# A fused attention and squared-ReLU block: activation sums on DVE alone, one product of seven by one step, and small products in the order of their weight blocks

## The chip, the core and the metric

The kernel runs on one core of a Trainium2 chip. The core has a matrix engine (PE, which loads weights and streams columns past them), a vector engine (DVE), an activation engine (ACT), a general engine (GpSimd, POOL in the profile) and a queue engine (SP) that issues nearly all transfers of this kernel. Each engine works through its own instructions in order and waits on semaphores for the others. The metric is the time of one execution on the device in microseconds, the median of several runs; lower is better.

## The reference

Attention without softmax, a norm, then a two-matrix block with a squared ReLU, all in float32:

```python
kv = np.einsum('bhsd,bhse->bhde', k, v)            # batch 8, heads 8, seq 576, head_dim 64
out = np.einsum('bhsd,bhde->bhse', q, kv)
rms = np.sqrt(np.mean(out * out, axis=-1, keepdims=True) + 1e-06)
x = (out / rms * g_norm)                           # to (4608 tokens, 512)
h = x @ w_in                                       # 512 x 2048
r = np.maximum(h, 0.0)
g = r * r
return g @ w_out                                   # 2048 x 512
```

## The kernel before

**Strips.** The 4608 tokens are 36 tiles of 128; four tiles make a strip, nine strips in all (0 to 8). Each strip has an up stage (x times W_in, ReLU, square, giving g) and a down stage (g times W_out). Slices of the attention for later strips (`attend`) are interleaved with the up stages. Program order is the order of each engine; nothing is reordered by a scheduler.

**Fast products.** A product of 2 x 2 blocks is made from seven block products P1 to P7 instead of eight (Winograd's form of Strassen), at the price of sums on either side. Strip 0 computes its up stage plainly; all others use seven products for each of four groups of columns (`up`). The down stage uses seven products in every strip. In strips 0 and 1 each of them is done by `down` in two halves of 8 matmuls on 256 columns. From strip 2 on (`DEEP` = 2) each of the seven is itself split into seven small products (`down_deep`, L753): two levels, 49 small products of four 128 x 128 x 128 matmuls. A float32 matmul stands as two instructions in the profile, so an outer product is 7 x 4 x 2 = 56 instructions there.

**A deep down stage.** The outer products run in the order 4, 1, 2, 6, 5, 7, 3. Product p needs:

- a quarter of g (`gq`, tile `gt`, 128 x 2048): quarters 11, 12, 21, 22. P4 and P5 read 22, P1 and P6 read 11, P2 and P3 read 21, P7 reads 12. Between products three of them are overwritten with the outer sums: 22 becomes 12 + 22 behind P4 (L764, DVE), 12 becomes 11 - 12 (L765, GpSimd), 11 becomes 22 - 11 behind P1 (L767, DVE), 21 becomes 21 - 11 behind P2 (L768, GpSimd).
- four leaf sums (`leaf_sums`, L707, tiles `g_s`, 128 x 512, DVE): s1 = a21 + a22, s2 = s1 - a11, s3 = a11 - a21, s4 = a12 - s2. Small products 1, 2 and 4 read quarters of the quarter as they are; 5, 6, 7, 3 read s1, s2, s3, s4.
- two blocks of weights, streamed by SP into a ring of four buffers (`stream`, L630): first the columns for small products 3, 1, 2, out of `w_out` (768 KB, L639), then those for 5, 6, 7, 4, out of `w_deep` (1 MB, L644). The ring is reused as PE releases a buffer.

The small products of one p are issued in two halves, (1, 2, 4) and then (5, 6, 7, 3) (L793). They accumulate in two PSUM banks, a chain: "A" for P1, P6, P7 and "B" (banks C and B) for P4, P2, P5, P3. P6, P7 and P3 go on accumulating onto the product before them in their chain. After the first half of product k, `together` (L736) adds the banks of product k - 1 into an output tile: one copy on ACT, then four adds on DVE reading PSUM, and where an output quarter is complete, one more add and the stores (`send`, L650), eight small DMAs on SP for most strips. Then the leaf sums for product k + 1 follow on DVE. Only after the second half are the blocks of two products ahead requested (`stream(2)`, L774), behind any stores in SP's order.

**Strip 0.** At the first down step (L806) the buffers of the weight conversion become those of the sums, `sums_g` (L576) for all four groups is issued (a sum for P5 and a difference for P7 each), and then the steps P1, P2, P5, P6, P7, P3, P4 run, with normalizations (`query`, `normalized`, L401) and transposes (`features`, L448) of later tiles between them. The difference for P6 is issued behind P1 (L674), that for P3 behind P2 (L678).

Of the kernel before, what the change touches and what calls it, by code (L numbers as in the profile page):

```python
# [14 lines left out]
ALU = mybir.AluOpType  # L15
# [4 lines left out]
def kernel(  # L20
# [34 lines left out]
    nc = tc.nc  # L55
    P = 128
    B, H, S, D = q.shape
# [5 lines left out]
    C = S // P  # L63
# [7 lines left out]
    N_STRIP = N_TILE // NT  # L71
# [168 lines left out]
    def minus(eng, out, a, b):  # L240
        eng.tensor_tensor(out=out, in0=a, in1=b, op=ALU.subtract)  # L241
# [235 lines left out]
    def sums_x(s):  # L477
        xc[s] = t1, t2, t3, t4 = [
            sum_pool.tile([P, TH // SQ, KH, SQ], FP32, name=f"x_t{i}", tag="sum") for i in range(4)
        ]  # L480
        x = lambda kh, th: halves(s, kh, th)
        minus(nc.vector, t1, x(0, 1), x(0, 0))
        minus(nc.vector, t2, x(1, 1), t1)
        minus(nc.vector, t3, x(1, 1), x(0, 1))
        minus(nc.vector, t4, x(1, 0), t2)
# [138 lines left out]
        w_blk[0, p] = t.rearrange("p f (h e) -> p h f e", h=2)  # L624
    DEEP_ORDER = (4, 1, 2, 6, 5, 7, 3)
    to_stream = [(s, p) for s in range(DEEP) for p in ORDER if (s, p) not in w_blk]
    to_stream += [(s, p, n) for s in range(DEEP, N_STRIP) for p in DEEP_ORDER for n in range(2)]
    to_stream = iter(to_stream)

    def stream(n=1):  # L630
        for _, u in zip(range(n), to_stream):
            s, p = u[:2]
            t = stream_pool.tile([P, 4, FQ // 2, P], FP32, name="w_blk", tag="w_blk")
            if s < DEEP:
                w_blk[u] = t.rearrange("p (h a) f e -> p h (a f) e", h=2)
                nc.sync.dma_start(out=w_blk[u], in_=w_out[B_OUT[p]])
            elif u[2] == 0:

                nc.sync.dma_start(  # L639
                    out=t[:, 1:4], in_=w_out[B_OUT[p]].rearrange("p h (a f) e -> p (h a) f e", a=2)[:, 1:4]  # L640
                )
                w_blk[s, p, 3], w_blk[s, p, 1], w_blk[s, p, 2] = (t[:, i] for i in range(1, 4))
            else:
                nc.sync.dma_start(out=t, in_=w_deep[B_OUT[p]])  # L644
                w_blk[s, p, 5], w_blk[s, p, 6], w_blk[s, p, 7], w_blk[s, p, 4] = (t[:, i] for i in range(4))

    def out_tile():
        return c_pool.tile([P, 2, DH], FP32, name="o_sb", tag="c")
# [6 lines left out]
    def down(s, p, i):  # L655
        if i == 0:
            open_bank(p)
        a = {1: 11, 2: 21, 6: 11, 7: 12, 3: 21, 4: 22}.get(p)
        w = w_blk[s, p]
        product(  # L660
            p, i,
            lambda fc: (gq[s, 1, fc // 2][:, fc % 2] if p == 5 else gq[s, a][:, fc])[:, ts(i, P)],
            lambda fc: w[:, :, fc], FQ,
        )
        if i == 0:
            if s == DEEP - 1:
# [24 lines left out]
        combine(p, store(0, 0), store(0, 1), store(1, 0), store(1, 1))  # L691
# [15 lines left out]
    def leaf_sums(s, p):  # L707
        a = gq[s, A_G[p]]
        a11, a12, a21, a22 = (a[:, ts(f, FQ // 2), ts(t, P)] for t in range(2) for f in range(2))
        s1, s2, s3, s4 = (sum_pool.tile([P, FQ // 2, P], FP32, name=f"g_s{i}", tag="sum") for i in range(4))  # L710
        leaf[p] = {1: a11, 2: a12, 3: s4, 4: a22, 5: s1, 6: s2, 7: s3}
        nc.vector.tensor_tensor(out=s1, in0=a21, in1=a22, op=ALU.add)  # L712
        minus(nc.vector, s2, s1, a11)
        minus(nc.vector, s3, a11, a21)
        minus(nc.vector, s4, a12, s2)


    PLACE = {1: (0, 0), 2: (0, 1), 6: (0, 2), 5: (1, 0), 7: (1, 1), 3: (1, 2), 4: (1, 3)}

    def small_products(s, p, js):  # L720
        c = "B" if p in (4, 2, 5, 3) else "A"
        if js[0] == 1 and p not in (6, 7, 3):
            chain[c] = [
                fpsum.tile([P, 4, P], FP32, name=f"ps_{c}", tag=t, bufs=2 if t == "A" else 1)
                for t in ("AA" if c == "A" else "CB")
            ]
        for j in js:
            x, i = PLACE[j]
            a, w = leaf[p][j], w_blk.pop((s, p, j))
            for f in range(FQ // 2):  # L730
                nc.tensor.matmul(  # L731
                    chain[c][x][:, i, :], lhsT=a[:, f, :], rhs=w[:, f, :],
                    start=p not in (6, 7, 3) and j in (1, 4) and f == 0, stop=f == FQ // 2 - 1, skip_group_check=True,
                )

    def together(p):  # L736

        x, y = chain["B" if p in (4, 2, 5, 3) else "A"]
# [3 lines left out]
        add = lambda out, a, b: nc.vector.tensor_tensor(out=out, in0=a, in1=b, op=ALU.add)  # L742
# [6 lines left out]
        for a, th, eh in {2: [(1, 0, 0)], 7: [(4, 1, 0), (5, 1, 1)], 3: [(6, 0, 1)]}.get(p, []):  # L749
            add(part[a], part[a], o)  # L750
            send(s, th, eh, part[a])

    def down_deep(s, k, js):  # L753
        p = DEEP_ORDER[k]
        small_products(s, p, js)
        before = DEEP_ORDER[k - 1] if k else None
        after = DEEP_ORDER[k + 1] if k < 6 else None
        g = lambda q: gq[s, q]
        if js[0] == 1:
            if k:  # L760
                together(before)
            if k == 0:
                leaf_sums(s, after)
                nc.vector.tensor_tensor(out=g(22), in0=g(12), in1=g(22), op=ALU.add)  # L764
# [12 lines left out]

    attend(ready[0] - 2)
    for i in range(NP, NP + 2):
# [2 lines left out]
    for s in range(N_STRIP):  # L782
# [6 lines left out]
        if s < DEEP:  # L789

            steps += [(2, down, (s, p, i)) for p in (ORDER if s else (1, 2, 5, 6, 7, 3, 4)) for i in range(2)]
        else:
            steps += [(2, down_deep, (s, k, js)) for k in range(7) for js in ((1, 2, 4), (5, 6, 7, 3))]  # L793
        goal = ready.get(s + 1, len(slices))
        total, done = sum(w for w, _, _ in steps), 0
        for i, (w, fn, a) in enumerate(steps):
            if s == 0 and i < n_up:

                convert(5 + (3 * i + 2) // 4)
                if i in (2, 4):  # L800
                    load_next()
                if i == 3:
                    load_q_rest(0, nc.sync)
                    load_rest(1, nc.sync)
                    load_q_rest(1, nc.sync)
# [12 lines left out]
            fn(*a)  # L818
            done += w
            if s:  # L820
# [52 lines left out]
```

## Time and profile before

| | us |
|---|---|
| median of 3 runs (1011.82 to 1011.95) | 1011.83 |
| the profiled execution | 1007.17 |
| its span, first to last instruction | 1005.4 |
| PE busy | 937.5 (93%) |
| DVE busy | 684.7 (68%) |
| ACT busy | 230.5 (23%) |
| GpSimd busy | 67.9 (7%) |

All times in views are microseconds from the start of the span. Busy time counts an instruction from its start to its modelled end; consecutive matmuls overlap, so start-to-start distances tell more than durations. A row of a wait names the engine that waited, what released it, the total, the times and the longest. The mean granted PE clock of the execution is 0.983 of full speed.

### The profile page before, as it was taken

How to read it: one execution, taken by the hardware profiler on the slowest of the kernel's cores; microseconds unless marked ns; L12 is line 12 of the kernel's file. 1: busy time of each engine (PE TensorE's matmuls, PEld its weight loads, DVE VectorE, ACT ScalarE, POOL GpSimd, SP SyncE). 2: the span in 40 equal slices, each digit the busy share in tenths (PEclk: the TensorE clock that was granted, in tenths of full speed). 3: DMA queues.
4: the chain of work that ended last, by engine and by line, in shares of the span. 5: the costliest groups of instructions: out<-in, count | busy, mean ns of one | idle time of the engine just before them, and what ended most of it. 6: DMA issues, size and time to landing. Idle time of an engine off the chain costs nothing.

```text
span 1005.4 us, 15784 instructions
## 1 busy us (share of the span) xinstructions
PE 937.5 (93%) x6144; PEld 828.0 (82%) x6144; DVE 684.7 (68%) x1203; ACT 230.5 (23%) x508; POOL 67.9 (7%) x21
## 2 busy tenths in 40 slices
PE   3699899999999999998999899989998999989995
PEld 3344788888889988898889888979898989988995
DVE  3899754585448974697569774986479557953593
ACT  3798241320022002200230022101220122002200
POOL 0000000000000300030002100110002000300030
PEclk9899999999999999999999999999999999989998
DMA  8699862546973566566555656466416721662064
GB/s 255 219 298 296 280 197 93 121 142 212 323 218 86 220 247 187 121 222 243 169 134 182 239 188 163 142 234 221 117 59 217 260 83 47 225 248 78 13 226 170
DMA packets 165530, 185.86 MB, mean 185 GB/s; under 512 B 85200, under 2 KB 138960, under 8 KB 156880
## 3 DMA queue, kind: packets, MB, share of 16 engines
q1 hardware_dynamic: 165296, 184.86, 57.2%
q8 instruction: 48, 0.79, 0.3%
q14 instruction: 26, 0.21, 0.1%
q10 hardware_dynamic: 160, 0.00, 0.0%
HBM read 153.62 MB, written 31.20 MB: 184 GB/s over the span
## 4 chain that ended last, share of the span: by engine, by line
PE 66%; DVE 23%; DMA 6%; issue 2%; ACT 2%; SPq 1%; DVEq 0%
PE ps_A L552 25%; PE ps_B L552 12%; DVE g_s L241 8%; PE ps_C L552 7%; PE ps_B L731 7%; PE ps_A L731 6%; DVE g_s L712 4%; DVE o_sb L742 3%; PE ps_A L588 2%; PE x_ps L378 2%; DMA w_blk<-w_out 2%; PE kv_ps L349 2%; DVE gt L241 2%; DVE gt L764 2%; DMA w_blk<-w_deep 1%
## 5 line engine op out<-in xcount | busy, mean ns | idle before, releaser
L552 PE MATMUL ps_A<-x_t,w_in 128*128 128x256 f32 x768 | 182.6, 381 | 1.3 <-DVE gt L611 1.3
L552 PEld LDWEIGHTS ps_A<-x_t,w_in 128*128 128x128 f32 x768 | 143.6, 190 | 21.1 <-DVE gt L611 2.1
L241 POOL TENSOR_TENSOR gt<-gt 128x2048 f32<-128x2048 f32 x14 | 66.2, 4726 | 902.0 <-DVE gt L764 856.6
L731 PE MATMUL ps_B<-w_blk,g_s 128*128 128x128 f32 x896 | 104.6, 275 | 0.0
L731 PEld LDWEIGHTS ps_B<-w_blk,g_s 128*128 128x128 f32 x896 | 102.3, 192 | 0.0
L731 PE MATMUL ps_A<-w_blk,gt 128*128 128x128 f32 x504 | 68.2, 297 | 21.6 <-DMA w_blk<-w_out 20.1
L731 PE MATMUL ps_A<-w_blk,g_s 128*128 128x128 f32 x672 | 80.5, 276 | 7.9 <-DVE g_s L241 7.9
L731 PEld LDWEIGHTS ps_A<-w_blk,g_s 128*128 128x128 f32 x672 | 77.5, 192 | 9.2 <-DVE g_s L241 9.2
L731 PEld LDWEIGHTS ps_A<-w_blk,gt 128*128 128x128 f32 x504 | 65.3, 211 | 23.2 <-issue 21.2
L731 PE MATMUL ps_B<-w_blk,gt 128*128 128x128 f32 x672 | 79.6, 275 | 0.0
L731 PEld LDWEIGHTS ps_B<-w_blk,gt 128*128 128x128 f32 x672 | 77.9, 192 | 0.4
L612 DVE SCALAR_TENSOR_TENSOR gt<-gt 128x512 f32<-128x512 f32 x96 | 66.4, 692 | 3.3
L562 ACT COPY snap<-ps_A 128x512 f32<-128x512 f32 x68 | 39.7, 584 | 116.9 <-PE ps_A L552 110.3
L241 DVE TENSOR_TENSOR g_s<-g_s,gt 128x512 f32<-128x512 f32 x49 | 63.3, 1291 | 1.7
L611 DVE TENSOR_TENSOR gt<-ps_C,snap 128x512 f32<-128x512 f32 x32 | 21.9, 684 | 60.6 <-PE ps_C L552 60.6
L611 DVE TENSOR_TENSOR gt<-ps_A,snap 128x512 f32<-128x512 f32 x32 | 22.0, 687 | 59.6 <-PE ps_A L552 59.5
L552 PE MATMUL ps_A<-xT,w_in 128*128 128x256 f32 x256 | 61.2, 382 | 0.0
L552 PE MATMUL ps_C<-xT,w_in 128*128 128x256 f32 x256 | 61.0, 381 | 0.0
L552 PE MATMUL ps_B<-x_t,w_in 128*128 128x256 f32 x256 | 60.9, 381 | 0.0
L552 PE MATMUL ps_B<-xT,w_in 128*128 128x256 f32 x256 | 60.7, 380 | 0.0
L742 DVE TENSOR_TENSOR o_sb<-o_sb,ps_A 128x256 f32<-128x256 f32 (+1 forms) x84 | 32.4, 386 | 38.8 <-ACT o_sb L743 28.4
L712 DVE TENSOR_TENSOR g_s<-gt 128x512 f32<-128x512 f32 x49 | 54.5, 1112 | 0.5
(118 smaller groups left out, 1284.5 us busy)
## 6 DMA issues: line engine op xcount, KB each, us to landing
w_blk<-w_deep SPq DMA_DIRECT2D x49, 1024.0 KB, 7.2
w_blk<-w_out SPq DMA_DIRECT2D x49, 768.0 KB, 4.5
w_blk<-w_out SPq DMA_DIRECT2D x11, 1024.0 KB, 6.4
raw<-in_moe_w_in_dram SPq DMA_DIRECT2D x16, 512.0 KB, 6.3
raw<-in_moe_w_out_dram SPq DMA_DIRECT2D x16, 512.0 KB, 5.1
k<-in_k_dram SPq DMA_DIRECT2D x30, 256.0 KB, 3.0
v<-in_v_dram SPq DMA_DIRECT2D x30, 256.0 KB, 3.3
w_deep<-w_t SPq DMA_DIRECT2D x7, 1024.0 KB, 8.5
```

The lines of the kernel that those rows point to most:

```text
L241: eng.tensor_tensor(out=out, in0=a, in1=b, op=ALU.subtract)
L349: nc.tensor.matmul(ps[ts(h, D)], lhsT=a, rhs=w, start=c == 0, stop=c == C)
L378: nc.tensor.matmul(o, lhsT=qT[b, p][:, c_b, :], rhs=kvd[b, p], start=True, stop=True)
L552: nc.tensor.matmul(bank[BANK[p]][:, i, :], lhsT=lhsT(k), rhs=rhs(k), start=p in (1, 5, 2) and i == 0 and k == 0, stop=k == n - 1, skip_gro ...
L562: nc.scalar.copy(snap[p], b)
L588: nc.tensor.matmul(ps, lhsT=w_in[:, kc % KH, g, kc // KH * 2 + fh, ts(i, P)], rhs=xt[0][:, :, kc, :], start=kc == 0, stop=kc == NP - 1,)
L611: nc.vector.tensor_tensor(out=o, in0=b, in1=a, op=ALU.add)
L612: nc.vector.scalar_tensor_tensor(out=o, in0=o, scalar=0.0, in1=o, op0=ALU.max, op1=ALU.mult)
L712: nc.vector.tensor_tensor(out=s1, in0=a21, in1=a22, op=ALU.add)
L731: nc.tensor.matmul(chain[c][x][:, i, :], lhsT=a[:, f, :], rhs=w[:, f, :], start=p not in (6, 7, 3) and j in (1, 4) and f == 0, stop=f == F ...
L742: add = lambda out, a, b: nc.vector.tensor_tensor(out=out, in0=a, in1=b, op=ALU.add)
L764: nc.vector.tensor_tensor(out=g(22), in0=g(12), in1=g(22), op=ALU.add)
```

## The change

1. `DEEP_ORDER` stays, but P2 is no longer split: it is done as in strips 0 and 1, by one step, 16 matmuls on 256 columns into bank C. Its weights come as one block of 1 MB from `w_out`; its four leaf sums and its `together` fall away, and its result is added to P1's output tile from bank C directly.
2. The two GpSimd subtractions are issued on DVE: 12 one product later than before (behind the combination of P4, at P1), 21 at P6.
3. The halves are (1, 2, 3) and (4, 5, 6, 7), so each half reads one block only. After every half the next load is requested, one at a time. In `leaf_sums`, s4 is computed ahead of s3. The sum for quarter 22 is issued behind the second half of P4.
4. In strip 0 the four `sums_g` are issued one in front of each of the first four down steps; the difference for P6 moves behind P2, that for P3 behind P5.

```diff
-    to_stream += [(s, p, n) for s in range(DEEP, N_STRIP) for p in DEEP_ORDER for n in range(2)]
+    for s in range(DEEP, N_STRIP):
+        for p in DEEP_ORDER:
+            to_stream += [(s, p, n) for n in range(2)] if p != 2 else [(s, p)]
...
-        if p == 1:
+
+        if p == (1 if s else 2):
             for g in range(NG):
                 x = gq[s, 11][:, ts(g, 2)]
                 minus(nc.vector, x, gq[s, 1, g], x)
-        if p == 2:
+        if p == (2 if s else 5):
             minus(nc.vector, gq[s, 21], gq[s, 21], gq[s, 11])
...
         minus(nc.vector, s2, s1, a11)
+        minus(nc.vector, s4, a12, s2)
         minus(nc.vector, s3, a11, a21)
-        minus(nc.vector, s4, a12, s2)
...
-        c = "B" if p in (4, 2, 5, 3) else "A"
+        c = "B" if p in (4, 5, 3) else "A"
...
-    def down_deep(s, k, js):
+    def down_deep(s, k, i):
         p = DEEP_ORDER[k]
-        small_products(s, p, js)
-        before = DEEP_ORDER[k - 1] if k else None
-        after = DEEP_ORDER[k + 1] if k < 6 else None
-        g = lambda q: gq[s, q]
-        if js[0] == 1:
-            if k:
-                together(before)
-            if k == 0:
-                leaf_sums(s, after)
-                nc.vector.tensor_tensor(out=g(22), in0=g(12), in1=g(22), op=ALU.add)
-                minus(nc.gpsimd, g(12), g(11), g(12))
-            if k == 2:
-                minus(nc.vector, g(11), g(22), g(11))
-                minus(nc.gpsimd, g(21), g(21), g(11))
-            if 0 < k < 6:
-                leaf_sums(s, after)
-            if k == 6 and s + 1 < N_STRIP:
-                sums_x(s + 1)
-        else:
-            stream(2)
+        if p == 2:
+            if i == 0:
+                open_bank(p)
+            w = w_blk[s, p]
+            product(p, i, lambda fc: gq[s, 21][:, fc, ts(i, P)], lambda fc: w[:, :, fc], FQ)
+        else:
+            small_products(s, p, ((1, 2, 3), (4, 5, 6, 7))[i])
+        if p != 2 or i == 1:
+            stream()
+        q11, q12, q21, q22 = (gq[s, q] for q in (11, 12, 21, 22))
+        if i == 1:
+            if k == 0:
+                nc.vector.tensor_tensor(out=q22, in0=q12, in1=q22, op=ALU.add)
             if k == 6:
-                together(p)
+                together(s, p)
+            return
+        if k == 3:
+            c11 = part[1]
+            nc.vector.tensor_tensor(out=c11, in0=c11, in1=bank["C"], op=ALU.add)
+            send(s, 0, 0, c11)
+        elif k:
+            together(s, DEEP_ORDER[k - 1])
+        if k == 0:
+            leaf_sums(s, 1)
+        if k == 1:
+            minus(nc.vector, q12, q11, q12)
+        if k == 2:
+            minus(nc.vector, q11, q22, q11)
+        if 2 <= k < 6:
+            leaf_sums(s, DEEP_ORDER[k + 1])
+        if k == 3:
+            minus(nc.vector, q21, q21, q11)
+        if k == 6 and s + 1 < N_STRIP:
+            sums_x(s + 1)
...
                 stream(3)
-                for g in range(NG):
-                    sums_g(0, g)
...
+            if s == 0 and n_up <= i < n_up + NG:
+                sums_g(0, i - n_up)
             fn(*a)
```

What the change moves stands in the order of the program at three places.

**PE, the first deep strip, product P1** (`w_blk_1920` is its block from `w_out`, `w_blk_1922` that from `w_deep`; `g_s0` to `g_s3` are s1 to s4). Before:

```order
L731 MATMUL ps_A_2378<-w_blk_1920,gt_1929 128x128 x8
L731 MATMUL ps_A_2379<-w_blk_1922,gt_1929 128x128 x4
L731 MATMUL ps_A_2379<-w_blk_1922,g_s0_2348 128x128 x4
L731 MATMUL ps_A_2378<-w_blk_1922,g_s1_2349 128x128 x4
L731 MATMUL ps_A_2379<-w_blk_1922,g_s2_2350 128x128 x4
L731 MATMUL ps_A_2379<-w_blk_1920,g_s3_2351 128x128 x4
```

After, with the first row of P2:

```order
L736 MATMUL ps_A_2377<-w_blk_1920,gt_1929 128x128 x8
L736 MATMUL ps_A_2378<-w_blk_1920,g_s3_2353 128x128 x4
L736 MATMUL ps_A_2378<-w_blk_1922,gt_1929 128x128 x4
L736 MATMUL ps_A_2378<-w_blk_1922,g_s0_2350 128x128 x4
L736 MATMUL ps_A_2377<-w_blk_1922,g_s1_2351 128x128 x4
L736 MATMUL ps_A_2378<-w_blk_1922,g_s2_2352 128x128 x4
L552 MATMUL ps_C_2418<-w_blk_2348,gt_1931 128x256 x16
```

The product with s4 moved from last to third, so the first block is read in the first three rows only; the second is read from the third small product's end on.

**SP, strip 4, from the load of the second block of P5 on.** Before, the stores of one output quarter stand ahead of both blocks of P7 and then both of P3:

```order
L644 DMA w_blk<-w_deep 128x2048
L653 DMA out_dram<-o_sb 32x256 x8
L639 DMA w_blk<-w_out 128x1536
L644 DMA w_blk<-w_deep 128x2048
L639 DMA w_blk<-w_out 128x1536
```

After, from the first block of P7 to its second, with what each waits for (DMAHW0 to DMAHW7 are the eight semaphores that SP's transfers use in turn):

```order
L641 DMA w_blk<-w_out 128x1536 [waits DMAHW4_49,DMAHW0_49,PE_49]
L657 DMA out_dram<-o_sb 32x256 [waits DMAHW5_49,DVE_49]
L657 DMA out_dram<-o_sb 32x256 [waits DMAHW6_49]
L657 DMA out_dram<-o_sb 32x256 x2
L657 DMA out_dram<-o_sb 32x256 [waits DMAHW1_49,Activation_49]
L657 DMA out_dram<-o_sb 32x256 [waits DMAHW2_49]
L657 DMA out_dram<-o_sb 32x256 [waits DMAHW3_49]
L657 DMA out_dram<-o_sb 32x256 [waits DMAHW4_49]
L647 DMA w_blk<-w_deep 128x2048 [waits DMAHW5_49,PE_49]
```

P7's first block moved ahead of the stores; the second stands behind them, and the eighth store waits on the semaphore of P7's first block (DMAHW4).

**DVE, strip 0, from the first sum on** (`g_s` is a sum of `sums_g`, the row below it the difference; `x_n` is the normalized tile that PE transposes). Before:

```order
L579 TENSOR_TENSOR g_s_960<-gt 128x512
L241 TENSOR_TENSOR gt<-gt 128x512
L579 TENSOR_TENSOR g_s_963<-gt 128x512
L241 TENSOR_TENSOR gt<-gt 128x512
L579 TENSOR_TENSOR g_s_966<-gt 128x512
L241 TENSOR_TENSOR gt<-gt 128x512
L579 TENSOR_TENSOR g_s_969<-gt 128x512
L241 TENSOR_TENSOR gt<-gt 128x512
L386 TENSOR_REDUCE ms<-sq 128x8
```

After:

```order
L579 TENSOR_TENSOR g_s_966<-gt 128x512
L241 TENSOR_TENSOR gt<-gt 128x512
L386 TENSOR_REDUCE ms<-sq 128x8
L387 TENSOR_SCALAR ms<-ms 128x8
L393 RECIPROCAL rms<-rms 128x8
L396 SCALAR_TENSOR_TENSOR newton<-ms,rms 128x8
L397 TENSOR_TENSOR newton<-newton,rms 128x8
L398 SCALAR_TENSOR_TENSOR rms<-newton,rms 128x8
L405 TENSOR_TENSOR x_n<-x_ps,rms 128x512
L579 TENSOR_TENSOR g_s_1001<-gt 128x512
```

The normalization of one tile moved from behind the fourth sum to in front of the second, and two more (not shown) stand in front of the third and the fourth.

More of the change, by code (lines that the diff above doesn't have):

```diff
@@ L631, in stream @@
         for _, u in zip(range(n), to_stream):
-            s, p = u[:2]
+            p = u[1]
             t = stream_pool.tile([P, 4, FQ // 2, P], FP32, name="w_blk", tag="w_blk")
-            if s < DEEP:
+            if len(u) == 2:
                 w_blk[u] = t.rearrange("p (h a) f e -> p h (a f) e", h=2)
@@ L641, in stream @@
                 )
-                w_blk[s, p, 3], w_blk[s, p, 1], w_blk[s, p, 2] = (t[:, i] for i in range(1, 4))
+                for i, j in enumerate((3, 1, 2)):
+                    w_blk[*u[:2], j] = t[:, i + 1]
             else:
                 nc.sync.dma_start(out=t, in_=w_deep[B_OUT[p]])
-                w_blk[s, p, 5], w_blk[s, p, 6], w_blk[s, p, 7], w_blk[s, p, 4] = (t[:, i] for i in range(4))
+                for i, j in enumerate((5, 6, 7, 4)):
+                    w_blk[*u[:2], j] = t[:, i]
     def out_tile():
@@ L732, in small_products, with together @@
                     chain[c][x][:, i, :], lhsT=a[:, f, :], rhs=w[:, f, :],
-                    start=p not in (6, 7, 3) and j in (1, 4) and f == 0, stop=f == FQ // 2 - 1, skip_group_check=True,
+                    start=p not in (6, 7, 3) and j in (1, 3) and f == 0, stop=f == FQ // 2 - 1, skip_group_check=True,
                 )
-    def together(p):
-        x, y = chain["B" if p in (4, 2, 5, 3) else "A"]
+    def together(s, p):
+        x, y = chain["B" if p in (4, 5, 3) else "A"]
         o = part[p] = out_tile()
@@ L747, in together @@
         add(q[:, 0:4:3], q[:, 0:4:3], y[:, 2:4])
-        for a, th, eh in {2: [(1, 0, 0)], 7: [(4, 1, 0), (5, 1, 1)], 3: [(6, 0, 1)]}.get(p, []):
+        for a, th, eh in {7: [(4, 1, 0), (5, 1, 1)], 3: [(6, 0, 1)]}.get(p, []):
             add(part[a], part[a], o)
             send(s, th, eh, part[a])
-    def down_deep(s, k, js):
+    def down_deep(s, k, i):
         p = DEEP_ORDER[k]
-        small_products(s, p, js)
-        before = DEEP_ORDER[k - 1] if k else None
-        after = DEEP_ORDER[k + 1] if k < 6 else None
-        g = lambda q: gq[s, q]
-        if js[0] == 1:
-            if k:
-                together(before)
-            if k == 0:
-                leaf_sums(s, after)
-                nc.vector.tensor_tensor(out=g(22), in0=g(12), in1=g(22), op=ALU.add)
-                minus(nc.gpsimd, g(12), g(11), g(12))
-            if k == 2:
-                minus(nc.vector, g(11), g(22), g(11))
-                minus(nc.gpsimd, g(21), g(21), g(11))
-            if 0 < k < 6:
-                leaf_sums(s, after)
-            if k == 6 and s + 1 < N_STRIP:
-                sums_x(s + 1)
-        else:
-            stream(2)
-            if k == 6:
-                together(p)
@@ L792 @@
         else:
-            steps += [(2, down_deep, (s, k, js)) for k in range(7) for js in ((1, 2, 4), (5, 6, 7, 3))]
+            steps += [(2, down_deep, (s, k, i)) for k in range(7) for i in range(2)]
         goal = ready.get(s + 1, len(slices))
```

## The prediction

> **What bounds the kernel now.** I read the list of waits first, because TensorE (PE) is busy 93% of the span: what it waited for in the middle of the program is nearly all there is to win.
>
> ```profile
> PE ps_A L731 <- DMA w_blk<-w_out: 20.1, 7, 3.6
> PE ps_A L731 <- DVE g_s L241: 8.3, 8, 1.2
> PE xt_ps L453 <- DVE x_n L405: 4.3, 1, 4.3
> ```
>
> Columns: who waited for whom, us in total, times, longest. Seven times PE waits for a block of W_out and about seven times for a leaf sum: once per deep strip (strips 2 to 8). The third row is one gap, in strip 0. So the next view is the table of windows, one per deep stage, from its first small product to its last.
>
> ```profile
> 324.44:372.39 47.95, 44.50 (x393) 43.99 (x392) 42.47 (x62) 3.09 (x9) 9.44 (x2) 1.00 0.65 238
> 428.07:476.70 48.63, 44.54 (x393) 44.03 (x392) 42.50 (x62) 3.09 (x9) 9.45 (x2) 1.00 0.65 235
> 532.67:582.32 49.65, 45.90 (x394) 45.55 (x393) 42.50 (x62) 3.09 (x9) 9.46 (x2) 0.97 0.63 231
> 637.95:688.62 50.67, 45.93 (x393) 45.58 (x392) 42.49 (x62) 3.08 (x9) 9.45 (x2) 0.97 0.63 228
> 744.59:794.64 50.05, 45.69 (x393) 45.34 (x392) 42.48 (x62) 3.08 (x9) 9.46 (x2) 0.97 0.63 230
> 847.46:899.08 51.62, 46.94 (x393) 46.58 (x392) 42.50 (x62) 3.09 (x9) 9.45 (x2) 0.93 0.60 222
> 947.44:996.34 48.90, 44.51 (x393) 43.96 (x391) 40.08 (x58) 3.09 (x9) 9.45 (x2) 1.00 0.55 199
> sum 347.47, PE 318.01 PEld 315.02 DVE 295.02 ACT 21.62 POOL 66.17; mean PE 45.43 PEld 45.00 DVE 42.15 ACT 3.09 POOL 9.45
> ```
>
> Columns: window, its length, busy time of PE, weight loads, DVE, ACT and GpSimd (POOL), the granted PE clock, the DMA share, GB/s. The seven stages take **347.47 us**; in four of them the clock also falls under 1.00. The timeline of PE in the third window (strip 4) shows where:
>
> ```profile
> 532.67 2.84 PE L731 MATMUL ps_B<-w_blk,gt 128*128 128x128 f32 x24
> 538.92 2.84 PE L731 MATMUL ps_A<-w_blk,gt 128*128 128x128 f32 x24
> ...
> 554.11 1.06 PE L731 MATMUL ps_A<-w_blk,g_s 128*128 128x128 f32 x8
> 556.32 2.94 PE L731 MATMUL ps_A<-w_blk,g_s 128*128 128x128 f32 x24 [1.15 <-DVE g_s L241]
> ...
> 568.11 4.54 PE L731 MATMUL ps_A<-w_blk,gt 128*128 128x128 f32 x24 [2.59 <-DMA w_blk<-w_out]
> ```
>
> An outer product P starts every 538.92 - 532.67 = **6.25 us** where nothing waits, so seven take 43.75. P6 (fourth) stops 1.15 us for a leaf sum, P7 (sixth) 2.59 us for its block, and its first 24 matmuls then take 4.54 us where others take 2.84: the slow clock. All of it goes into the difference 347.47 - 7 x 43.75 = 41.2 us.
>
> Why these two stops? For P6, the groups of DVE and GpSimd by shape:
>
> ```profile
> L241 DVE TENSOR_TENSOR g_s<-g_s,gt 128x512 f32<-128x512 f32 x49 | 63.3, 1291 | 1.7
> L712 DVE TENSOR_TENSOR g_s<-gt 128x512 f32<-128x512 f32 x49 | 54.5, 1112 | 0.5
> L241 DVE TENSOR_TENSOR g_s<-gt,g_s 128x512 f32<-128x512 f32 x49 | 33.5, 683 | 0.0
> L764 DVE TENSOR_TENSOR gt<-gt 128x2048 f32<-128x2048 f32 x7 | 16.0, 2284 | 0.0
> L241 POOL TENSOR_TENSOR gt<-gt 128x2048 f32<-128x2048 f32 x14 | 66.2, 4726 | 902.0 <-DVE gt L764 856.6
> ```
>
> Four leaf sums have one shape; two of them average 1291 and 1112 ns, the others 683. In the timeline of strip 3 one such sum is not 0.69 but 4.89 us long, just when GpSimd does its 128x2048 subtraction:
>
> ```profile
> 446.76 4.89 DVE L241 TENSOR_TENSOR g_s<-g_s,gt 128x512 f32<-128x512 f32 x1
> ```
>
> So the excess, (608 + 429) ns x 49 = 51 us, is DVE held up by 14 GpSimd subtractions of 4.73 us, about 7.3 us a strip. For P7, the queue of SP in strip 4:
>
> ```profile
> 559.85 3.60 SPq L653 DMA_DIRECT2D out_dram<-o_sb  x8
> 563.55 0.37 SPq L639 DMA_DIRECT2D w_blk<-w_out  x1
> 564.01 0.38 SPq L644 DMA_DIRECT2D w_blk<-w_deep  x1
> ```
>
> P7's two blocks stand behind eight stores of finished output, which themselves waited for DVE. Their buffers were free from 559.0, where P6 ended (556.32 + 24 x 0.1116, a product's 6.25 us over its 56 matmuls). They start 4.5 us late, and PE waits 2.59 us for the first.
>
> **The change, part by part.** (1) *P2 by one step.* It replaces 56 matmul instructions of 128 columns by 32 of 256. That product exists in strip 0:
>
> ```profile
> 149.48 7.07 PE L552 MATMUL ps_B<-w_blk,gt 128*128 128x256 f32 x32
> 156.38 7.07 PE L552 MATMUL ps_A<-w_blk,gt 128*128 128x256 f32 x32
> ```
>
> Start to start 156.38 - 149.48 = 6.90, say 6.91 us: **+0.66 us** a strip against 6.25, on the path, +4.6 in all. Here a rule speaks differently. The Trainium skill, TensorE: Matmul & The Clock Gate, section Back-to-back issue gap, gives a sustained spacing of about 81 ns for 128 columns and 131 for 512; an estimate between them puts 256 columns at 1.21 times 128, so P2 would take 4.3 us and the sum be 18 us lower. The trace has 215.6 against 111.6 ns, 1.93 times, and decides; as a rival the rule's 951 us gets 0.01.
>
> (2) *GpSimd's two subtractions go to DVE.* DVE's busy time in a strip: 42.5, less 7.3 of hold-up, less four sums of P2 at 0.68 (2.7), plus 2 x 2.28: about 37.1 us of a stage of 44.4; P2's combination of five adds is replaced by one and not even counted. In order of time: a product's sums stand behind the combination of the product two ahead of it, of which three adds come after that product's last matmul (here P7 of the last strip):
>
> ```profile
> 990.29 1.20 DVE L742 TENSOR_TENSOR o_sb<-o_sb,ps_A 128x256 f32<-128x256 f32 x3 [1.07 <-PE ps_A L731]
> ```
>
> That is some 1.4 us, and then at most one 2.28 us subtraction. The new order needs the sum s4 after the first two small products, 16/56 x 6.25 = 1.79 us into a product. The sums s1, s2, s4 (2.05 us) are then ready at 1.4 + 2.28 + 2.05 = 5.7 us after the start of the product ahead, and needed at 6.25 + 1.79 = 8.0: 2.3 us spare. So the 1.15 us stop goes, and nothing is late next on DVE. If that cover failed, the price would be today's 1.3 us a strip, 8 to 9 us.
>
> (3) *Blocks fetched ahead.* A first half now uses only the block of W_out and a second half only that of W_deep, so each half frees its buffer, and twelve loads start an outer product earlier relative to their use. In a strip with P4 at 0 and P1, P2, P6, P5, P7 at 6.25, 12.5, 19.41, 25.66, 31.91: P7's first block starts when P6's first half ends, 22.1 + 0.2, and is needed at 31.91. P7's second block is the tight one: it stands behind eight stores, and as the order shows, each DMA waits on the semaphore of the eighth before it, so the eighth store waits until P7's first block has landed (strips 4 to 8; strips 2 and 3 have five and six stores there).
>
> ```profile
> DMA to landing us min/median/max: 4.2/4.5/8.8
> DMA to landing us min/median/max: 5.9/7.2/11.1
> ```
>
> (First row: loads of L639, 768 KB; second: L644, 1 MB.) 22.3 + 4.5 = 26.8, a store 0.5, hence 27.5 or so; landing at 27.5 + 5.9 to 7.2 = 33.4 to 34.7; needed at 31.91 + 2.68 = 34.6. Today's 7.2 us is with a 768 KB load under way 0.9 us ahead; here that load has landed, so I take the 5.9 end: about a microsecond spare. By the median it would be late by 0.1 us, by the maximum by 4. Other second blocks are requested as one product ends and needed one product and 2.68 us later, 8.9 us. P2 takes 1 MB instead of 1.75; that saving I cost at nothing, since no transfer is then waited for.
>
> So a deep stage becomes 6 x 6.25 + 6.91 = 44.41 us, seven 310.9: **-36.6 us** against 347.47, the slow clock behind the gaps included.
>
> (4) *Strip 0, sums spread over four steps.*
>
> ```profile
> 109.51 1.05 PE L378 MATMUL x_ps<-kv_all,qT 128*128 128x128 f32 x8
> 114.90 1.11 PE L453 MATMUL xt_ps<-ident,x_n 128*128 128x128 f32 x4 [4.34 <-DVE x_n L405]
> 115.81 4.72 PE L552 MATMUL ps_C<-w_in,gt 128*128 128x256 f32 x16
> ...
> 121.26 3.62 PE L552 MATMUL ps_C<-w_in,gt 128*128 128x256 f32 x16
> 124.71 0.60 PE L453 MATMUL xt_ps<-ident,x_n 128*128 128x128 f32 x4
> ```
>
> ```profile
> 106.09 0.60 ACT L384 ACTIVATE sq<-x_ps 128x512 f32<-128x512 f32 x1 [3.09 <-PE x_ps L373]
> ```
>
> ```profile
> 108.09 0.69 DVE L579 TENSOR_TENSOR g_s<-gt 128x512 f32<-128x512 f32 x1 [3.49 <-DMA w_out<-wt]
> 112.09 0.68 DVE L386 TENSOR_REDUCE ms<-sq 128x8 f32<-128x512 f32 x1
> 114.15 0.69 DVE L405 TENSOR_TENSOR x_n<-x_ps,rms 128x512 f32<-128x512 f32 x1
> ```
>
> DVE waits for a store to free a buffer for the second sum; the normalization that PE wants stands behind four sums. In the new order it stands ahead of the second: it takes 114.84 - 112.09 = 2.75 us, its input, the squares of ACT, exists at 106.7, so it ends near 109.5, before PE asks (109.51 + 0.89 = 110.4). The gap of 4.34 goes, the transposes behind it take 0.60 instead of 1.11, and the half of P2 that took 4.72 takes 3.62: 4.34 + 0.5 + 1.1 = **-5.9 us**. The sums (1.3 us a pair) then come between normalizations of 2.75; the fourth pair follows the third normalization, whose PE input ends near 115.3, so it is ready near 120.2, and P5, which starts there, reaches it after three quarters of its first 3.46 us, near 122.7. The subtractions moved behind P2 and P5 are read by P6 and P3, one product of 6.9 us later or more, and take 2.5 and 2.28 us. A bound from the other side: none gained, if P5 stops for the fourth sum.
>
> **Sum.** 36.6 + 5.9 = 42.5. The profiled execution took 1007.17 us (span 1005.4), so 964.7; the timed runs have a median of 1011.83, 4.66 above it. I carry the saving over unchanged: **969.3 us**. If those 4.66 us are more gaps of the same kind, they go too, and it is 964.7.
>
> **Rivals.** *P7's second block is late (0.14).* The wait has moved from the first block to the second, by the hold on the eighth store. For it: the spare microsecond; against: fewer loads compete. At 2 us late (between the 0.1 and the 4 above) in the five strips with eight stores, plus a slow clock behind it of 4.54 - 2.84 = 1.7, 18.5 us return: 988.
>
> ```profile
> 983.10 2.02 PE L731 MATMUL ps_A<-w_blk,gt 128*128 128x128 f32 x16 [2.84 <-DMA w_blk<-w_out]
> ```
>
> That slow clock is not sure: a gap of 2.84 us left 16 matmuls at full pace (2.02), one of 2.59 did not. The same page of the Trainium skill, Part 1, puts the drop behind an idle window of about 3.4 us; by that rule such gaps would cost 10 us in all, 979. The 2.59 us row disagrees with it.
>
> The price stays the dearer one.
>
> *Strip 0 gives nothing (0.07)*: the wait moves to P5; 969.3 + 5.9 = 975.
>
> *DVE's long sums are not GpSimd's doing (0.03)*: then 7.3 us a strip stay and DVE is busy 42.5 - 3.8 + 4.6 = 43.3 of 44.4; P6 keeps its stop of 1.3: 978. Against it: two of four equal sums run at 683.
>
> *The loads starve PE (0.04)*, the slower case: every block is now requested singly, and if W_deep's loads land in 11 us, the maximum above, instead of 5.9 to 7.2, the three with a lead of 8.9 us are each 2.1 us late and slow PE by 1.7 more: 3 x 3.8 x 7 = 80 us, 1049. It loses from a landing of about 9.2 us on: (0.3 + 1.7) x 21 = 42. Against it: a strip loads 11.5 MB in 44.4 us where it loaded 12.25 in 49.65, a rate only 5% higher, and today's 7.2 us is the median of loads that follow another at once.
>
> *It hides nothing (0.02)*: PE finds another wait of the same size; 1010 to 1013.
>
> **How the numbers follow.** The forecast has 0.69, between 964 and 974. About 0.2% is what a measurement of this kernel tells from no change. Faster: 0.69 + 0.14 + 0.07 + 0.03 + 0.01 (the rule on 256 columns) = 0.94; same 0.02; slower 0.04. The range for 8 in 10 starts at 963.5 (all 4.66 us go, and a little) and ends at 984, which takes in the two middle rivals and the milder half of the first.
>
> **What would show it.** Right: the seven stages at 44.4 us each, PE with no wait for a leaf sum or for W_out, clock 1.00; sums at 0.68 us throughout; no 4.34 us gap near 110. Wrong: a wait of PE for W_deep in P7 (the first rival), a wait for s4 at the third small product of P6 or P7, P2 far from 6.9 us, or a new wait in an up stage, from stores that SP issues later.

## The result, and the profile after

The changed kernel takes **964.49 us** (median of 4 runs, 963.25 to 967.63) against 1011.83 for the kernel before (median of 4, 1009.62 to 1011.95): ratio **0.9542**, 95% interval 0.9514 to 0.957. The profiled execution took 963.43 us (before 1007.17), its span 961.6 (before 1005.4), its granted clock 0.993 (before 0.983).

What PE waits for, all rows over 1 us, in the list of waits of the changed kernel (who waited, for whom, total, times, longest):

```profile
PE t_ps L331 <- DMA q<-in_q_dram: 10.5, 1, 10.5
PE xt_ps L440 <- DVE x_n L430: 6.3, 3, 4.7
PE x_ps L419 <- ACT kv_all L352: 3.7, 4, 1.7
PE ps_A L552 <- DVE gt L611: 1.3, 2, 0.6
```

The three rows that opened the prediction are gone; the first three here belong to the start of the program. The windows of the deep stages (window, length, busy time of PE, weight loads, DVE, ACT, GpSimd, clock, DMA share, GB/s), the first, the last and the sum of seven:

```profile
317.27:361.69 44.42, 44.42 (x369) 43.59 (x368) 36.67 (x56) 2.82 (x8) 0.00 (x0) 1.00 0.72 255
...
908.21:952.62 44.41, 44.41 (x369) 43.57 (x367) 34.16 (x52) 2.82 (x8) 0.00 (x0) 1.00 0.56 201
sum 310.90, PE 310.90 PEld 305.06 DVE 254.11 ACT 19.73 POOL 0.00; mean PE 44.41 PEld 43.58 DVE 36.30 ACT 2.82 POOL 0.00
```

Length and PE's busy time are equal: PE never stops in a deep stage, and the clock is 1.00. They take 347.47 - 310.90 = 36.6 us less. The leaf sums on DVE, by shape:

```profile
L241 DVE TENSOR_TENSOR g_s<-gt,g_s 128x512 f32<-128x512 f32 x42 | 29.1, 692 | 1.4
L241 DVE TENSOR_TENSOR g_s<-g_s,gt 128x512 f32<-128x512 f32 x42 | 29.1, 692 | 1.4
L717 DVE TENSOR_TENSOR g_s<-gt 128x512 f32<-128x512 f32 x42 | 28.8, 687 | 0.5
```

None is held up any more. Strip 0, in the timeline of PE (start, length):

```profile
109.65 0.60 PE L453 MATMUL xt_ps<-ident,x_n 128*128 128x128 f32 x4
110.09 3.62 PE L552 MATMUL ps_C<-w_in,gt 128*128 128x256 f32 x16
...
127.90 4.27 PE L552 MATMUL ps_A<-w_blk,gt 128*128 128x256 f32 x19
```

P6 starts at 127.90 (before 134.72), 6.8 earlier, of which some 0.7 were there already ahead of the gap (100.53 against 101.27 for the same step), in code that the change does not touch. The span's 43.8 us are thus 36.6 in the deep stages, 6.1 in strip 0 and about 1 elsewhere.

### The profile page after: what moved, and what is told of

The parts are those of the page before. It is cut to its first block, busy times and chain, and to the rows that moved or that the text cites. A ratio compares the mean times of both kernels' runs of the same rounds, so it can differ in the third digit from the quotient of the medians.

```text
span 961.6 us, 15319 instructions
## 1 busy us (share of the span) xinstructions
PE 930.4 (97%) x5976; PEld 819.1 (85%) x5976; DVE 643.8 (67%) x1161; ACT 228.7 (24%) x501; POOL 1.7 (0%) x7
## 4 chain that ended last, share of the span: by engine, by line
PE 95%; ACT 2%; DVE 1%; DMA 1%; SPq 0%; issue 0%; DVEq 0%
PE ps_A L552 29%; PE ps_B L552 14%; PE ps_B L736 14%; PE ps_A L736 14%; PE ps_C L552 12%; PE ps_A L588 3%; PE x_ps L378 3%; PE kv_ps L349 2%; PE ps_B L588 1%; PE ps_C L588 1%; DMA raw<-in_moe_w_in_dram 1%; PE x_ps L419 0%; PE x_ps L373 0%; PE xt_ps L440 0%; ACT raw L206 0%; ACT w_c L203 0%
## 5 line engine op out<-in xcount | busy, mean ns | idle before, releaser
L736 PE MATMUL ps_B<-w_blk,g_s 128*128 128x128 f32 x672 | 81.9, 275 | 0.0
L736 PEld LDWEIGHTS ps_B<-w_blk,g_s 128*128 128x128 f32 x672 | 78.4, 192 | 0.0
L736 PE MATMUL ps_B<-w_blk,gt 128*128 128x128 f32 x504 | 63.1, 275 | 0.0
L736 PE MATMUL ps_A<-w_blk,gt 128*128 128x128 f32 x504 | 63.1, 275 | 0.0
L241 DVE TENSOR_TENSOR gt<-gt 128x2048 f32<-128x2048 f32 (+1 forms) x31 | 58.1, 1873 | 4.0 <-PE ps_C L552 3.8
L736 PEld LDWEIGHTS ps_A<-w_blk,gt 128*128 128x128 f32 x504 | 60.2, 192 | 0.4
L736 PEld LDWEIGHTS ps_B<-w_blk,gt 128*128 128x128 f32 x504 | 60.2, 192 | 0.4
L552 PE MATMUL ps_C<-w_blk,gt 128*128 128x256 f32 x256 | 56.6, 379 | 0.0
L552 PEld LDWEIGHTS ps_C<-xT,w_in 128*128 128x128 f32 x256 | 48.1, 190 | 6.7 <-issue 0.2
L552 PEld LDWEIGHTS ps_B<-xT,w_in 128*128 128x128 f32 x256 | 48.3, 190 | 6.5
```

What stands on the lines that cost most here:

```text
L552: nc.tensor.matmul(bank[BANK[p]][:, i, :], lhsT=lhsT(k), rhs=rhs(k), start=p in (1, 5, 2) and i == 0 and k == 0, stop=k == n - 1, skip_gro ...
L736: nc.tensor.matmul(chain[c][x][:, i, :], lhsT=a[:, f, :], rhs=w[:, f, :], start=p not in (6, 7, 3) and j in (1, 3) and f == 0, stop=f == F ...
```

## The experiments

The forecast was met; the question left was which part of the change does it. The deep stages have three edits: P2 in one step or split, the two subtractions on DVE or GpSimd, the loads with the new halves or the old ones. All eight combinations ran, all with strip 0's new order, the later places of the subtractions and s4 ahead of s3. One place differs between the halves of the table: with P2 split, 21 - 11 is issued at P5, one product later than in the changed kernel.

| P2 | subtractions | halves, loads | run | seven deep stages, us | median, us | ratio to before, 95% |
|---|---|---|---|---|---|---|
| one step | DVE | new | changed kernel, e11 | 310.9 | 964.5 | 0.9534 (0.9513 to 0.9556) |
| one step | DVE | old | e2 | 311.7 | 964.9 | 0.9552 (0.9539 to 0.9565) |
| one step | GpSimd | new | e3 | 310.9 | 964.3 | 0.9544 (0.9531 to 0.9557) |
| one step | GpSimd | old | e5 | 311.1 | 966.5 | 0.9553 (0.9523 to 0.9583) |
| split | DVE | new | e4, e12 | 306.3 | 959.1 | 0.9476 (0.9456 to 0.9496) |
| split | DVE | old | e6 | 316.3 | 969.6 | 0.9586 (0.9568 to 0.9604) |
| split | GpSimd | new | e7 | 349.3 | 1003.1 | 0.9915 (0.9896 to 0.9934) |
| split | GpSimd | old | e10 | 351.8 | 1006.2 | 0.9949 (0.993 to 0.9969) |

The stages are the sums of the windows in each profile, 347.5 for the kernel before; the time of the split, DVE, new row is that of e12, beside e11 on the same chip.

**e1: the subtractions alone.** On the kernel before:

```diff
-                minus(nc.gpsimd, g(12), g(11), g(12))
+                minus(nc.vector, g(12), g(11), g(12))
...
-                minus(nc.gpsimd, g(21), g(21), g(11))
+                minus(nc.vector, g(21), g(21), g(11))
```

> The kernel before with one edit: its two GpSimd subtractions a deep strip go to DVE, at the same place in the order. Theory A (the prediction's): two separate causes. DVE's long sums make P6's stop, loads that stand behind eight stores make P7's. Then here the sums fall to 0.69 us and P6's stop goes (8 to 9 us), but P7's two blocks are still requested only after the stores, so most of its 20 us of waits and the slow clock behind them stay: about -10 us, some 1000. Theory B: the hold-up of DVE makes both, since the stores wait for DVE's combinations; then the stores leave SP's queue before P6 ends, both stops go, seven deep stages take 43.75 us each, and the time falls by about 41 us, to some 966 to 971.

990.93 us, ratio 0.9816 (0.9794 to 0.9839): between the two. P6's stops are gone, P7's stay. In strip 4, from the timelines of PE, DVE and SP's queue:

```profile
547.62 2.84 PE L731 MATMUL ps_A<-w_blk,gt 128*128 128x128 f32 x24
...
562.58 4.54 PE L731 MATMUL ps_A<-w_blk,gt 128*128 128x128 f32 x24 [2.29 <-DMA w_blk<-w_out]
```

```profile
543.85 4.68 DVE L241 TENSOR_TENSOR gt<-gt 128x2048 f32<-128x2048 f32 x2
```

```profile
553.45 3.98 SPq L653 DMA_DIRECT2D out_dram<-o_sb  x8
557.52 0.37 SPq L639 DMA_DIRECT2D w_blk<-w_out  x1
```

P2 ends where P6 starts, at 547.62; the eight stores start 5.8 us later, behind two subtractions (4.68 us), P6's sums and P2's combination on DVE, and P7's block comes after them. So SP's delay is DVE's backlog handed on, whatever makes the backlog. e6 makes the same three choices with other places: the subtractions behind the leaf sums, 12's one product and 21's two products later than here, and the sum for quarter 22 behind P4's second half. It needs 316.3 us for the seven stages where this run needs 330.2: these places and s4 ahead of s3 are together worth 13.9 us.

**e2 and e3: one remedy undone.** On the changed kernel, e2:

```diff
-            small_products(s, p, ((1, 2, 3), (4, 5, 6, 7))[i])
-        if p != 2 or i == 1:
-            stream()
+            small_products(s, p, ((1, 2, 4), (5, 6, 7, 3))[i])
+        if i == 1:
+            stream(1 if p == 2 else 2)
```

> The changed kernel with the old halves (1,2,4 and 5,6,7,3) and both blocks requested after a product's second half, so that nothing is fetched an outer product ahead; subtractions on DVE and P2 in one step stay. Theory A (the prediction's): PE stops for P7's block again in every deep strip, 1 to 3 us and in several strips the slow clock behind it: +14 to +30 us, some 978 to 994. Theory B (DVE's hold-up made both stops, the order of the loads adds nothing): no stop over 0.3 us, within 1 or 2 us of the changed kernel, 963 to 966.

e3:

```diff
-            minus(nc.vector, q12, q11, q12)
+            minus(nc.gpsimd, q12, q11, q12)
...
-            minus(nc.vector, q21, q21, q11)
+            minus(nc.gpsimd, q21, q21, q11)
```

> The changed kernel with its two subtractions (g11 - g12 beside P1, g21 - g11 beside P6) back on GpSimd. Theory A: one DVE operation beside each subtraction grows from 0.69 to 3.6 to 4.9 us; the one beside P1 is covered, since P2 needs no leaf sums, the one beside P6 meets P5's sums (2.3 us spare in the new order, and the subtraction itself no longer on DVE): a stop of 1 to 2 us a strip at P5, or stores so late that P7's second block comes late: +5 to +20 us. Rival: all covered now, since the new order leaves room; 963 to 966, and then moving the subtractions to DVE was not needed.

964.9 and 964.3 us: each rival held, theory A fell twice. Undoing either costs under 1 us. In e3 the hold-up has not gone away; the timelines of GpSimd and DVE in strip 4:

```profile
525.30 4.52 POOL L241 TENSOR_TENSOR gt<-gt 128x2048 f32<-128x2048 f32 x1 [83.49 <-DVE gt L772]
537.67 4.53 POOL L241 TENSOR_TENSOR gt<-gt 128x2048 f32<-128x2048 f32 x1 [7.85 <-PE ps_C L552]
```

```profile
525.07 1.71 DVE L747 TENSOR_TENSOR o_sb<-o_sb,ps_B 128x256 f32<-128x256 f32 x4
530.07 0.42 DVE L747 TENSOR_TENSOR o_sb<-o_sb,ps_A 128x256 f32<-128x256 f32 x1 [3.28 <-ACT o_sb L748]
...
538.18 4.57 DVE L717 TENSOR_TENSOR g_s<-gt 128x512 f32<-128x512 f32 x1
...
543.50 0.69 DVE L241 TENSOR_TENSOR g_s<-gt,g_s 128x512 f32<-128x512 f32 x1
```

The first subtraction now falls where P2's leaf sums would have stood: DVE sits idle there for 3.28 us and nothing is held. The second still stretches a sum from 0.69 to 4.57 us, but it is P5's s1, and no backlog stands ahead of it: s4 (last row) is there at 544.2, and P5, which starts 25.66 us into the stage, at 543.6, wants it 1.79 us later, at 545.4.

**e5: both undone.** The diffs of e2 and e3 together.

> The changed kernel with both undone: the two subtractions on GpSimd and the old halves and requests of the loads; P2 in one step and strip 0's order stay. The two runs that undid one of them stood within 0.5 us of the changed kernel. Theory C (either remedy does, the other is spare): without both, P7's stop is back, 1 to 3 us a strip with the slow clock behind: 975 to 994. Theory D (P2 in one step is the remedy: c11 is finished by one addition right behind P2, so the stores leave SP's queue before P6 ends, and P2's four leaf sums are gone): no stop over 0.3 us, 964 to 967.

966.46 us: theory D. The deep stages take 311.1 us, no stop; the median's 2 us over the changed kernel are outside them (its list of waits has 2.4 us for W_out, both stops in strip 1). SP's queue in strip 4, where P2 ends at 541.1 (19.41 us into the stage) and P6 at 547.4:

```profile
541.34 0.32 SPq L647 DMA_DIRECT2D w_blk<-w_deep  x1
542.06 4.71 SPq L657 DMA_DIRECT2D out_dram<-o_sb  x8
546.87 0.37 SPq L641 DMA_DIRECT2D w_blk<-w_out  x1
```

The stores begin 0.9 us after P2 ends, behind one addition (5.8 us in e1), and P7's block is requested while P6 still runs.

**e4 and e12: P2 split, all else as changed.** On the changed kernel (without the branch for P2 and the single addition that completes the output quarter c11, and with P2's bank and chain as before):

```diff
-            to_stream += [(s, p, n) for n in range(2)] if p != 2 else [(s, p)]
+            to_stream += [(s, p, n) for n in range(2)]
...
+        small_products(s, p, ((1, 2, 3), (4, 5, 6, 7))[i])
+        stream()
...
-        if k == 1:
-            minus(nc.vector, q12, q11, q12)
         if k == 2:
             minus(nc.vector, q11, q22, q11)
-        if 2 <= k < 6:
+        if k < 6:
             leaf_sums(s, DEEP_ORDER[k + 1])
-        if k == 3:
+        if k == 1:
+            minus(nc.vector, q12, q11, q12)
+        if k == 4:
             minus(nc.vector, q21, q21, q11)
```

> The changed kernel with P2 again by seven small products (two more loads' worth of W: 1.75 MB instead of 1 MB for P2, four more leaf sums and a full combination), in the new halves, with all sums on DVE: g11 - g12 behind P2's sums, g21 - g11 one product later. Theory A: P2 in one step costs 0.66 us a deep strip on PE and nothing waits in its place, so splitting it gives 7 x 0.66 = 4.6 us: about 4.6 below the changed kernel, some 959 to 960; DVE would be busy about 41 of 43.75 us. Rival: P2 in one step bought slack that the rest needs (DVE 36.7 of 44.4 us, one load fewer); split, PE stops for a leaf sum or a block of P2 or P6 in every strip, 1 to 3 us each: 965 to 985.

> The changed kernel once more, on the same chip as the next run: 963 to 967.

> The kernel with P2 by seven small products, new halves and all sums on DVE, once more, beside the changed kernel: 4.6 us below it by 7 x 0.66 us of P2; if that was chance, within 2 us of it.

e4 959.7 us; again beside the changed kernel, e12 959.1 (958.71 to 959.84) against e11 964.5 (962.95 to 966.61), and the intervals of their ratios do not meet. Theory A held: the windows of e12, first and sum,

```profile
317.31:361.07 43.76, 43.76 (x393) 43.76 (x392) 40.44 (x64) 3.09 (x9) 0.00 (x0) 1.00 0.78 275
...
sum 306.33, PE 306.33 PEld 306.30 DVE 280.55 ACT 21.61 POOL 0.00; mean PE 43.76 PEld 43.76 DVE 40.08 ACT 3.09 POOL 0.00
```

show 310.9 - 306.3 = 4.6 us from P2, PE without a stop, and DVE at 40.4 of 43.8 us. **This version beats both kernels**, 0.9476 of the time before.

**e6, e7, e10: with P2 split, the other two undone** (the diffs of e2 and e3 on e4).

> The run with P2 by seven small products (959.7 us), with the old halves and requests; sums all on DVE. Theory D: the stores of c11 now wait for P2's combination and the sums ahead of it on DVE, some 5 us after P2's end instead of 0.7, eight stores take 3.5 more, so P7's first block is requested some 9 us after P2's end and lands at 13.5, needed at 12.5: a stop of about 1 us in five to seven strips, with the slow clock behind some: 966 to 980. Rival (the loads need no fetch ahead at all while DVE is free of the hold-up): 959 to 961.

> The run with P2 by seven small products (959.7 us), with the two subtractions back on GpSimd; new halves and loads stay. Theory D: the 3.9 us hold-up of one sum now meets a DVE that has no step without leaf sums; P6 or P5 stops 1 to 3 us a strip: 968 to 985. Rival (new halves and fetch ahead cover it): 959 to 961.

> The run with P2 by seven small products (959.7 us), with both others undone: subtractions on GpSimd and old halves and requests. Against the kernel before it has strip 0's order and the later place of the two subtractions. Theory D: stops at P6 and P7 as before, 1003 to 1007, the kernel before less strip 0's 6 us. Rival: worse than the run with new halves and GpSimd (1003) by the 10 us that the old requests cost beside DVE, 1010 to 1014.

e6 969.62 us: 10 us come back, the size that theory D gave. The block is another one: theory D had P7's first block late, but the largest row is P7's second, from `w_deep`, in five of the seven strips.

```profile
PE ps_A L736 <- DMA w_blk<-w_deep: 3.8, 5, 1.4
```

Smaller rows of the deep stages, for W_out, W_deep at P3 and results of DVE, add 2.7 us. e7 1003.13, far worse than the 968 to 985 expected. Its list of waits, then strip 4 on GpSimd, DVE and PE:

```profile
PE ps_A L736 <- DVE g_s L241: 28.1, 7, 4.0
```

```profile
548.25 4.92 POOL L241 TENSOR_TENSOR gt<-gt 128x2048 f32<-128x2048 f32 x1 [6.61 <-ACT o_sb L748]
```

```profile
548.12 0.69 DVE L717 TENSOR_TENSOR g_s<-gt 128x512 f32<-128x512 f32 x1
548.84 4.88 DVE L241 TENSOR_TENSOR g_s<-g_s,gt 128x512 f32<-128x512 f32 x1
```

```profile
554.50 1.16 PE L736 MATMUL ps_A<-w_blk,g_s 128*128 128x128 f32 x8 [4.03 <-DVE g_s L241]
555.50 1.80 PE L736 MATMUL ps_A<-w_blk,gt 128*128 128x128 f32 x8
557.09 3.77 PE L736 MATMUL ps_A<-w_blk,g_s 128*128 128x128 f32 x24
```

P2's sums, themselves held up by the first subtraction, push P6's sums into the second; s2 ends at 553.72, and s4, which the new halves need first, after it. PE stops 4.03 us and then runs slow (1.80 for 1.06, 3.77 for 2.84): 349.3 - 306.3 = 43 us in seven stages. e10, with the old halves as well, takes 1006.19 us, as theory D said. From its list of waits:

```profile
PE ps_A L736 <- DVE g_s L241: 15.2, 15, 4.0
PE ps_A L736 <- DMA w_blk<-w_out: 9.9, 5, 3.3
```

P6's stops are shorter than in e7 (11.2 us of the first row; its longest wait, 4.0 us, stands at the start of P7 in strip 7), and P7's are back. Its median is 5.8 us below that of the kernel before in the same series (1011.96), yet its deep stages are 4.4 us longer (351.8 against 347.5): the new places and s4's order by themselves do not help the deep stages, and the gain lies outside them.

**e8: strip 0 undone.** On the changed kernel:

```diff
                 stream(3)
+                for g in range(NG):
+                    sums_g(0, g)
...
-            if s == 0 and n_up <= i < n_up + NG:
-                sums_g(0, i - n_up)
...
-        if p == (1 if s else 2):
+        if p == 1:
...
-        if p == (2 if s else 5):
+        if p == 2:
```

> The changed kernel with strip 0 as it was (its eight sums together ahead of the first down step, the subtractions one product earlier); deep strips as changed. Theory A (the prediction's): the gap of 4.3 us near 110 and what it slows come back: +5.9 us, some 970.4. Rival (strip 0 gives nothing, the wait only moved): within 1 us of the changed kernel.

972.92 us (970.82 to 975.91), 8.4 above the changed kernel: theory A, more than its 5.9. The timeline of PE has the gap back, 6.16 us instead of 4.34:

```profile
116.16 1.11 PE L453 MATMUL xt_ps<-ident,x_n 128*128 128x128 f32 x4 [6.16 <-DVE x_n L405]
117.07 4.81 PE L552 MATMUL ps_C<-w_in,gt 128*128 128x256 f32 x16
```

The size of this gap varies: e1 and e9, which keep strip 0 as it was, have 5.8 and 5.0 us there. Beside it, PE waits 2.2 us for W_out in strip 1 in e8; with strip 0's new order e5 has 2.4 us of the same kind and the changed kernel none, so this part need not be strip 0's doing.

**e9: P2 in one step, alone, on the kernel before.**

```diff
-        small_products(s, p, js)
+        if p == 2:
+            i = js[0] // 5
+            if i == 0:
+                open_bank(p)
+            w = w_blk[s, p]
+            product(p, i, lambda fc: gq[s, 21][:, fc, ts(i, P)], lambda fc: w[:, :, fc], FQ)
+        else:
+            small_products(s, p, js)
```

> The kernel before with one edit: P2 of a deep strip in one step (one load of 1 MB, no leaf sums, c11 by one addition). Subtractions on GpSimd at their old places, old halves and requests, strip 0 as before. Theory D (P2 in one step is the remedy; strip 0 apart): the seven deep stages at 44.4 us each, no stop for a leaf sum or a block, strip 0's gap of 4 to 6 us still there: about 6 above the run with P2 in one step and both other edits undone (966.5), 970 to 974. Theory E (the edits only work together; without the later place of the subtractions, P6's sums are still held up): P6 stops about 1 us a strip and P7 behind it, 980 to 1000.

1025.3 us, ratio 1.0129 (1.0108 to 1.0151): both theories fell. At its old place the subtraction 21 - 11 is issued between P2's halves, so the second half multiplies 21 - 11 and not 21, and PE must wait for GpSimd (list of waits):

```profile
PE ps_C L552 <- POOL gt L241: 35.8, 7, 5.1
```

Split, the four sums of P2 had been taken from 21 before it was overwritten; in one step both halves read it. So the edit needs the later subtraction, and e5 is the smallest version tried that has it.

## Why the prediction was right, and where it was not

**The sum** held: the profiled saving is 43.7 us for a forecast of 42.5. The deep stages gave 36.6 for 36.6; strip 0 gave 6.1 for 5.9, and e8 confirms the sign and rough size. The deep stages' figure does not confirm the three remedies one by one: 44.41 us is the time of a stage without a stop, whichever remedy takes the stops away.

**The 4.66 us between the profiled and the timed runs before** were carried over, which put 969.3 in place of 964.5. The measured medians do what the prediction set down as the other case: they go too. This was the mis-sized term: the timed saving is 47.3, and the result lies at the low end of the 964 to 974 that the prediction held likeliest. The clock points to gaps of the same kind: the ten timed runs of the kernel before beside e1 have a granted clock of 0.977 to 0.983, the profiled one 0.983, the four runs of the changed kernel 0.992 to 0.994. One such gap is strip 0's: 4.34 us in the profile before, but 5.0 to 6.2 in the three later profiles with the old order (e1, e8, e9). What the 4.66 us are made of in the timed runs is not shown.

**(1) P2 by one step** was priced right and its role wrong. Start to start it takes 537.14 - 530.24 = 6.90 us in strip 4, and against the split version it costs 4.6 us in all, as forecast:

```profile
530.24 7.07 PE L552 MATMUL ps_C<-w_blk,gt 128*128 128x256 f32 x32
537.14 1.95 PE L736 MATMUL ps_A<-w_blk,gt 128*128 128x128 f32 x16
```

The prediction booked it as a cost on PE; on DVE it counted the four sums that fall away, and left P2's shorter combination "not even counted". The runs show that with the two other edits absent it is itself the cure, beside the later places: 351.8 to 311.1 us (e10, e5). It leaves DVE idle where the first subtraction runs (e3), and the stores leave 0.9 us after P2 (e5). By the estimate worked out from the figures of the Trainium skill, TensorE: Matmul & The Clock Gate, section Back-to-back issue gap, the one step would be the cheaper form; e12 answers that too: going back to 56 instructions of 128 columns took 4.6 us off the deep stages.

**(2) Subtractions to DVE.** The cost was right: DVE is busy 36.7 us in a stage (forecast 37.1), sums at 0.69. That P6's stop goes because of it is the step that failed as an explanation: with P2 in one step, GpSimd can keep them (e3, e5). With P2 split it is the large remedy, 351.8 to 316.3 (e10, e6).

**(3) Blocks fetched ahead.** P7's second block was less tight than feared. SP's queue in strip 4, and the landing of its third row:

```profile
540.02 0.32 SPq L641 DMA_DIRECT2D w_blk<-w_out  x1
540.43 4.27 SPq L657 DMA_DIRECT2D out_dram<-o_sb  x8
544.79 0.37 SPq L647 DMA_DIRECT2D w_blk<-w_deep  x1
```

```profile
DMA to landing us min/median/max: 5.0/5.0/5.0
```

Requested 27.1 us into the stage (forecast 27.5 or so), landed at 549.8, needed at 549.65 + 2.68 = 552.3: 2.5 us spare for a forecast of about one; the first rival did not come up. But again the credit was misplaced. The prediction saw that the stores ahead of the loads had waited for DVE, yet went after the order of the loads. The stores start 8.4 us after P2's end in the kernel before (559.85 against 532.67 + 3 x 6.25), 5.8 in e1 and 0.9 in e5, and with P2 in one step the old order of the loads costs under 1 us (e2, e5). It earns 10 us only with P2 split and the sums on DVE (e6, e4).

So the three edits are in part spare to one another. Beside the later places, P2 in one step cures the stage without the two others; without it, the two others are needed together and then give 4.6 us more.

Left open: the places of the subtractions and of the sum for quarter 22 and the order of s4 and s3 were not tried apart, and their 13.9 us come from two runs that also differ in strip 0, outside the windows compared. Each comparison of P2 in one step with P2 split also moves 21 - 11 by one product; what that alone does was not tried.

## What to carry to other kernels

When several edits are each aimed at a stop, their forecast savings may be right in sum and wrong one by one: run the combinations, because one edit that relieves the engine behind all the stops can make the others spare, and then its own price can be taken back. Before a queue's order is blamed for a late load, look at when its neighbours became ready: here the stores that held up the loads were waiting for a backlog on DVE. An operation overwritten in place ties its position to every later reader; merging a product's halves moved such a reader.

## What the runs showed of the hardware

A DVE leaf sum, which has two SBUF inputs, that starts while a GpSimd subtraction runs ends 0.55 us after it, whatever its own start (0.54 to 0.56 in all 56 cases of the kernel before, e3, e5, e7 and e10): in e7 548.84 + 4.88 = 553.72 against 548.25 + 4.92 = 553.17, in e3 542.75 against 542.20. The sum that had started before the subtraction, at 548.12 in e7, takes the usual 0.69. DVE additions that read PSUM beside the first subtraction of a strip are not held: 1.71 us for four at 525.07 in e3, as elsewhere. The Trainium skill, SBUF — State Buffer, section SBUF: two separate sides, describes the pair of ports that DVE and GpSimd share as a lock held for a whole instruction, which blocks the other; the trace agrees.

The length of a gap alone does not decide whether the slow clock follows. In e1 a gap of 2.29 us was followed by it (4.54 us for 24 matmuls that take 2.84 elsewhere), and a longer one was not (2.02 us for 16, the full pace):

```profile
666.92 2.02 PE L731 MATMUL ps_A<-w_blk,gt 128*128 128x128 f32 x16 [2.89 <-DMA w_blk<-w_out]
```
